# A three-stage kernel: when a gated layer's weights are converted, and in what order

## The chip, the cores and the metric

The kernel runs on one core of a Trainium2 chip. The metric is the device time of one execution in microseconds (us). TensorE (PE) multiplies, VectorE (DVE), ScalarE (ACT) and GpSimd (POOL) work on the elements, and SyncE (SP) issues most of the transfers. Each engine takes its instructions in the order in which they were written; an instruction that waits holds up all behind it on its engine.

## What is computed

Three layers follow each other: causal attention with a cumulative bias, a layer of eight experts (each token goes to one), and a gated layer. The change touches the last one and its surroundings.

```
# x: [2304, 512] from the attention, float32
for e in range(8):                       # w1: [8, 512, 1024], w2: [8, 1024, 512]
    out[mask_e] = gate_w[mask_e] * (relu(x[mask_e] @ w1[e]) @ w2[e])
gate = 1 / (1 + exp(-(out @ w_gate)))    # w_gate, w_val: [512, 1536], float64
val = out @ w_val
y = (gate * val) @ w_out                 # w_out: [1536, 512], float64
```

The three weights of the gated layer come as float64 and are turned into float32 on the chip.

## The kernel before

**Conversion.** `Decode` turns a block of float64 into float32 in four steps on three engines: `near` on POOL (`dn`, line 849) limits the exponent's byte, `far` on DVE (`dd`, 853) takes the difference, `word` on ACT (`ds` or `wr`, 857) writes it as the top of a 32-bit word, and `tail` on DVE (861) puts the mantissa under it. The raw block is tile `dr`, with two buffers; `load` issues the next block's transfer when a block is done.

**Precision.** Products are made from two reduced-precision parts each (high and low): ACT rounds a value to its high part, DVE or POOL subtracts to get the low one, and PE multiplies high by high, high by low and low by high.

**Experts.** Nine slots of 256 tokens, eight steps each. A step of PE makes one block of the hidden layer (`ph`, line 973) and multiplies the block before by w2 (993); ACT and DVE make `hH` and `hL` from `ph`; ACT, DVE and POOL split the weights of three steps further on (`w`, 906 and 909). Then two half-filled slots, four steps each, in plain float32: `half` (1094) transposes the hidden block on PE (`hth`), DVE copies it (`hT`, 1079), and PE multiplies by w2 (1088). `Moe.run` calls `step(u)` after each step, and a table `todo` in the main function says which pieces of the gated layer's preparation are written there.

**Gated layer.** `Moe2` works in units: a block of 512 columns pair by pair (f, six of them), a third of the tokens (t), gate or value (m): 36 units. A unit is a Strassen-like scheme of seven products, `slot` 0 to 6, six matmuls of 384 columns each. Its inputs are the sums of x blocks `a` (lines 1247 to 1249 make seven of them from four raw blocks `xs`, high and low), and of weight blocks `set` (1283 to 1289, from the converted `ds`). ACT copies partial sums out of bank X (`p`, `u`, line 1320), which PE adds to afterwards. `result` writes the gate (`sg`) or the product, which goes to DRAM (`h`, 1340). A dictionary in `run` places the tasks behind slots: `spread(first, last, tasks)` divides a list of them evenly.

**Final product.** `final` (1442) multiplies h, loaded again (`hr`) and split (`hl`, 1430 and 1431), by w_out (`po`), in 72 steps of nine matmuls. Before, the blocks 0 to 2 of w_out are converted in the last units, 3 to 11 from the last unit but one on, one after the other: `load_o` loads five raw blocks (`wr`), and each block's `low` loads the one five further on (line 1404).

Of the kernel before, what the change touches and what calls it, by code (L numbers as in the profile page):

```python
# [815 lines left out]
class Decode:  # L816
# [7 lines left out]
    def __init__(self, tc, pool, srcs):  # L824
        self.nc, self.pool, self.srcs = tc.nc, pool, srcs
        self.raw, self.n, self.i = {}, 0, 0

    def load(self):

        if self.n < len(self.srcs):  # L830
            src = self.srcs[self.n]
            c, w = src.shape[1:]
            t = self.raw[self.n] = self.pool.tile([128, 2048], U8, tag="dr", name="dr", bufs=2)
            self.nc.sync.dma_start(t.rearrange("p (c b) -> p c b", c=c)[:, :, :w], src)
            self.n += 1

    def tasks(self, dst):

        i = self.i
        self.i += 1  # L840
        return self.steps(lambda: self.raw[i], dst, 256) + [lambda: (self.raw.pop(i), self.load())]

    def steps(self, raw, dst, n):
        nc, V, o = self.nc, self.nc.vector, {}
        top = lambda: raw().bitcast(I8).rearrange("p (a b) -> p a b", b=8)[:, :, 4]

        def near():
            o["n"] = self.pool.tile([128, 512], I8, tag="dn", name="dn", bufs=1)[:, :n]
            nc.gpsimd.tensor_scalar(o["n"], top(), 56.0, -56.0, ALU.min, ALU.max)  # L849

        def far():
            o["d"] = self.pool.tile([128, 512], I8, tag="dd", name="dd", bufs=1)[:, :n]
            V.scalar_tensor_tensor(out=o["d"], in0=top(), scalar=-72.0, in1=o["n"], op0=ALU.max, op1=ALU.subtract)  # L853

        def word():
            o["t"] = dst().bitcast(I32)
            nc.scalar.activation(o["t"], o["d"], AF.Copy, scale=float(1 << 27))

        def tail():
            w = raw().bitcast(I32).rearrange("p (a b) -> p a b", b=2)[:, :, 0]  # L860
            V.scalar_tensor_tensor(out=o["t"], in0=w, scalar=5, in1=o["t"], op0=ALU.logical_shift_right, op1=ALU.bitwise_or)  # L861
# [340 lines left out]
class Moe2:  # L1202
# [10 lines left out]
    def __init__(self, tc, moe, x2, ids2, wg, wv, wo, out, hd, keep, rp):  # L1213
        self.tc, self.nc, self.moe = tc, tc.nc, moe
        self.x2, self.ids2, self.out, self.hd = x2, ids2, out, hd
        self.keep, self.rp, self.r = keep, rp, moe.r
# [3 lines left out]
        srcs = [cols(w, f, j, l).rearrange("(c p) b -> p c b", p=128) for f in range(self.NF) for w in (wg, wv) for j, l in blocks]  # L1220
        self.wo = wo.bitcast(U8)
        srcs += [self.wo[128 * f : 128 * f + 128, 2048 * h + 3 : 2048 * h + 2048].rearrange("(c p) b -> p c b", c=1) for f in range(3) for h in range(2)]
        self.dec = Decode(tc, keep, srcs)

# [10 lines left out]
    def load_x(self, t, pool, raws):  # L1235
# [430 lines left out]
```

## Time and profile before

| | us |
|---|---|
| three runs | 1053.5, 1055.35, 1057.93 |
| median | 1055.35 |
| profiled execution | 1056.42 |
| its span, first to last instruction | 1054.3 |
| PE busy | 958.7 (91%) |
| DVE busy | 633.5 (60%) |
| ACT busy | 536.6 (51%) |
| POOL busy | 420.3 (40%) |
| PE's mean granted clock | 0.957 of full |

A share of the whole span says little here, since the three layers have different limits; the stages are read one by one. A row of the timeline is one or more instructions of one kind: start, duration, engine, line, output and input, count, and in brackets the idle time before it and the engine and line that ended it. A matmul's end is modelled, so the time from one start to the next is the better measure of PE's pace.

### The profile page before, as it was taken

What the parts mean: (1) busy time and instruction counts of PE and PEld (TensorE: products, weight loads), DVE (VectorE), ACT (ScalarE), POOL (GpSimd) and SP (SyncE); (2) the same over time, 40 slices, a digit from 0 to 9 for tenths busy, and PEclk for the clock granted to TensorE, in tenths of its full rate; (3) what the DMA queues carried; (4) which work ended last, traced back from release to release, by engine and by line L of the source; (5) the groups of instructions that cost most, each with busy time, mean ns of one, the idle gap of its engine ahead of it and who ended that gap; (6) DMA issues with size and microseconds to landing.
All of it is one profiled execution on the core that took longest, in us unless ns stands there. A gap on an engine that the chain in (4) does not pass through costs nothing. (4 is left out here: it accounts for less than half of the span.)

```text
span 1054.3 us, 18246 instructions
## 1 busy us (share of the span) xinstructions
PE 958.7 (91%) x5937; PEld 866.1 (82%) x5937; DVE 633.5 (60%) x1535; ACT 536.6 (51%) x1317; POOL 420.3 (40%) x642
## 2 busy tenths in 40 slices
PE   7999999998879999999874889999999965899996
PEld 6888888876769999999864788999999954688885
DVE  6899989998565445554163766657576544523320
ACT  6988888887335555555133444353444433322220
POOL 7978697878545556665000000000000023311111
PEclk9999999999889999999987999999999988899998
DMA  6665467885351125115653322314233245434420
GB/s 161 155 136 136 114 78 150 139 99 200 35 62 58 41 81 179 43 41 150 196 165 93 111 67 74 117 62 140 85 109 100 78 165 191 155 130 135 140 76 30
DMA packets 149649, 117.99 MB, mean 112 GB/s; under 512 B 86946, under 2 KB 135357, under 8 KB 149543
## 3 DMA queue, kind: packets, MB, share of 16 engines
q1 hardware_dynamic: 144534, 106.28, 38.9%
q0 software_dynamic: 3792, 10.14, 3.2%
q8 instruction: 49, 0.80, 0.4%
q14 instruction: 58, 0.47, 0.2%
q10 hardware_dynamic: 1216, 0.30, 0.1%
HBM read 112.81 MB, written 29.04 MB: 135 GB/s over the span
## 5 line engine op out<-in xcount | busy, mean ns | idle before, releaser
L1311 PE MATMUL X<-a,set 128*128 128x384 f32 x864 | 173.7, 348 | 26.2 <-ACT u L1320 17.4
L1311 PEld LDWEIGHTS X<-a,set 128*128 128x128 f32 x864 | 155.3, 194 | 34.9 <-ACT u L1320 20.9
L849 POOL TENSOR_SCALAR dn<-dr 128x256 int8<-128x256 int8 x54 | 23.1, 427 | 321.9 <-DVE dd L853 208.6
L1442 PE MATMUL acc<-wo,hl 128*128 128x512 f32 x369 | 91.0, 403 | 14.5 <-ACT hl L1430 13.2
L909 POOL TENSOR_TENSOR w<-raw,w 128x512 fp32r<-128x512 f32 x56 | 78.4, 1410 | 59.1 <-ACT w L906 59.0
L1442 PEld LDWEIGHTS acc<-wo,hl 128*128 128x128 f32 x369 | 70.6, 193 | 32.8 <-ACT hl L1430 14.5
L170 POOL TENSOR_SCALAR bias<-cumB,cumT 128x576 f32<-128x576 f32 (+4 forms) x155 | 82.3, 533 | 37.5 <-DVE nm L289 31.3
L973 PE MATMUL ph<-xT,w 128*128 128x256 f32 x672 | 92.0, 287 | 1.9 <-DVE w L909 1.9
L298 ACT ACTIVATE P<-P,nm 64x64 f32<-64x64 f32 (+4 forms) x160 | 89.7, 564 | 2.9 <-DVE nm L289 2.8
L973 PEld LDWEIGHTS ph<-xT,w 128*128 128x128 f32 x672 | 85.4, 194 | 2.1 <-DVE w L909 2.1
L1311 PE MATMUL Y<-a,set 128*128 128x384 f32 x432 | 82.1, 338 | 0.4 <-DVE a L1248 0.4
L289 DVE CUSTOM_DVE_ANT_0 P<-sb,bias 128x576 f32<-128x576 f32 (+4 forms) x160 | 72.0, 479 | 17.1 <-PE sb L280 11.0
L339 DVE TENSOR_TENSOR PL<-pt,PH 128x512 fp32r<-128x512 f32 (+3 forms) x160 | 78.8, 530 | 3.4 <-ACT PH L331 2.5
L1311 PEld LDWEIGHTS Y<-a,set 128*128 128x128 f32 x432 | 76.6, 190 | 0.8 <-DVE a L1248 0.7
L331 ACT CAST PH<-pt 128x512 fp32r<-128x512 f32 (+3 forms) x160 | 66.9, 466 | 10.2 <-PE pt L317 7.3
L977 ACT ACTIVATE hH<-ph 128x256 fp32r<-128x256 f32 x72 | 27.7, 385 | 86.2 <-PE ph L973 79.6
L317 PE MATMUL pt<-ident,P 128*128 128x128 f32 (+2 forms) x480 | 70.0, 277 | 0.8 <-DVE PL L339 0.7
L978 DVE SCALAR_TENSOR_TENSOR hL<-ph,hH 128x256 fp32r<-128x256 f32 x72 | 30.5, 424 | 58.9 <-ACT hH L977 53.3
L909 DVE TENSOR_TENSOR w<-raw,w 128x512 fp32r<-128x512 f32 x56 | 54.3, 972 | 17.0 <-ACT w L906 14.1
L1449 POOL DMA_INDIRECT out_dram<-oy,row x18 | 19.2, 1068 | 111.4 <-ACT oy L1448 107.7
L906 ACT CAST w<-raw 128x512 fp32r<-128x512 f32 x112 | 63.6, 621 | 0.0
L317 PEld LDWEIGHTS pt<-ident,P 128*128 128x128 f32 (+2 forms) x480 | 53.4, 132 | 12.0 <-issue 6.3
(280 smaller groups left out, 2279.5 us busy)
## 6 DMA issues: line engine op xcount, KB each, us to landing
raw<-in_moe_w_dram SPq DMA_DIRECT2D x80, 512.0 KB
h<-sg SPq DMA_DIRECT2D x72, 192.0 KB
hr<-h SPq DMA_DIRECT2D x72, 192.0 KB
cumB<-cum_d SPq DMA_DIRECT2D x32, 288.0 KB
qraw<-in_q_dram SPq DMA_DIRECT2D x58, 128.0 KB
dr<-in_moe_w_gate_dram SPq DMA_DIRECT2D x24, 255.2 KB
dr<-in_moe_w_val_dram SPq DMA_DIRECT2D x24, 255.2 KB
x<-yt SPq DMA_DIRECT2D x9, 512.0 KB
```

The costliest lines, as they stand in the source:

```text
L170: (nc.vector if n in FILLB else nc.gpsimd).tensor_scalar(res[i][:rows], cumB[:rows, :m], -1.0, self.cumT[:rows, i, n : n + 1], ALU.mult, A ...
L289: nc.vector.tensor_tensor_reduce(out=pt[:rows], in0=self.sb[:rows, o : o + m], in1=self.bias_t[n][i][:rows], op0=ALU.add, op1=ALU.min, sca ...
L298: nc.scalar.activation(h["P"][i][:rows], h["P"][i][:rows], AF.Exp, bias=h["nm", i][:rows], scale=-1.0, accum_out=self.sums_t[(n // 2) % 3] ...
L317: nc.tensor.transpose(pt[: TS[j], c : c + TS[i]], h["P"][i][: TS[i], T0[j] : T0[j] + TS[j]], self.ident[: TS[i], : TS[i]])
L331: nc.scalar.copy(t[:r, a:z], pt[:r, a:z])
L339: nc.vector.tensor_tensor(t[:r, a:z], pt[:r, a:z], h["H"][u][:r, a:z].bitcast(F32), ALU.subtract)
L906: nc.scalar.copy(v, src)
L909: (eng or nc.vector).tensor_tensor(v, src, h.bitcast(F32), ALU.subtract)
L973: nc.tensor.matmul(ph, w[:, 128 * dc : 128 * dc + 128], x[:, dc], start=k == 0, stop=k == 11)
L978: nc.vector.scalar_tensor_tensor(out=hL, in0=ph, scalar=0.0, in1=hH.bitcast(F32), op0=ALU.max, op1=ALU.subtract)
L1311: self.nc.tensor.matmul(bank, w[:, c], a[:, h, c], start=first and k == 0, stop=k == 5, skip_group_check=True)
L1442: nc.tensor.matmul(self.acc[t], h[:, a, 128 * t : 128 * t + 128], w, start=f == 0 and k == 0, stop=f == 11 and k == 2)
```

## The change

Four things change.

1. **w_out is converted during the expert slots.** All twelve blocks are loaded, converted (512 columns at a time, three raw buffers) and stored to a DRAM tensor `wo32` as float32. In the end they are loaded from there, split into high and low, and used; no conversion is left in the last units.
2. **The first gate and value weights are converted there too**, behind the blocks of w_out, not among the half-filled experts.
3. **The steps of a conversion lie apart**: `stages` returns `near`, `far`, `word` and `tail`, each written behind a slot of its own, two conversions interleaved; the load of the next raw block follows `tail`. Buffers of `dn` and `dd` go from one to two. The second set's sums are all made in the first unit.
4. **Loads and stores are reordered**: the raw x of both remaining thirds is loaded at the start of the units; a store of h is written one slot later; eight blocks of h are loaded ahead of the final product instead of four; every second low half of w_out is made on DVE instead of POOL.

```
     def last_weight(self, pool):
+        dec = Decode(self.tc, pool, 512, [self.wo[128 * f : 128 * f + 128, 3:].rearrange("(c p) b -> p c b", c=1) for f in range(12)], 3)
+        for _ in range(3):
+            dec.load()
+        new = lambda: pool.tile([128, 512], F32, tag="dt", name="dt", bufs=2)
+        return [dec.stages(new, lambda t, f=f: self.nc.sync.dma_start(self.wo32[128 * f : 128 * f + 128, :], t)) for f in range(12)]
...
+        for k, stages in enumerate(glu.last_weight(pool(wo_ctx, "dec", side="right", reuse_waits="tile"))):
+            for i, task in enumerate(stages):
+                put(2 * k + i - 55, [task])
+        put(-28, [wo_ctx.close, open_xs, glu.dec.load, glu.dec.load])
+        (d0, s0), (d1, s1) = glu.w_tasks(0, lambda: xs[0]), glu.w_tasks(1)
+        for k, stages in enumerate(d0 + d1):
+            for i, task in enumerate(stages):
+                put(2 * k + i - 27, [task])
...
-                2: x[:4], 3: x[4:9] + d0[:5], 4: x[9:13] + d0[5:15], 5: x[13:] + d0[15:], 6: s0 + b0 + d1[:5], 7: d1[5:] + s1, 8: [glu.preload],
+            put(3, x[:4])
+            put(4, x[4:7] + s0[0])
...
-            for m, first, last in ((0, (b + (4 if f == 1 else 3), 5), (b + 5, 5)), (1, (b + 6, 5), (b + 8, 4))):
-                spread(first, last, [x for w in self.w_tasks(m) for x in w])
+            for m, soon, there in ((0, at(b + 1, 5), at(b + (4 if f == 1 else 3), 5)), (1, at(b + 4, 5), at(b + 6, 5))):
...
+                for stages, k in zip(blocks, (0, 1, 7, 8)):
+                    for i, task in enumerate(stages):
+                        put(soon + k + i, [task])
...
-        spread((n - 2, 4), (n - 2, 4), [lambda: [self.load_o(f) for f in range(3, 8)]])
-        spread((n - 2, 6), (n - 1, 3), ot[3] + ot[4])
+        put(at(n - 2, 5), [self.load_o])
+        put(at(n - 1, 0), [lambda: [self.load_h(0, f) for f in range(8)]])
```

What this does to the order is shown at three places. First, DVE among the half-filled experts, before; `a` and `xs` are x's high-low work, `hT` is the copy that PE waits for, `dd` and `ds` are a conversion:

```order
L1071 COPY xTh<-htr 128x512
L1248 TENSOR_TENSOR a_0_8774<-xs_8770,a_0_8774 128x768
L1079 COPY hT<-hth 128x256
L1248 TENSOR_TENSOR a_2_8776<-xs_8771,a_2_8776 128x768
L1249 TENSOR_TENSOR xs_8771<-xs_8773,xs_8771 128x768
L1248 TENSOR_TENSOR a_1_8775<-xs_8772,a_1_8775 128x768
L1249 TENSOR_TENSOR xs_8773<-xs_8770,xs_8773 128x768
L1249 TENSOR_TENSOR xs_8770<-xs_8771,xs_8770 128x768
L853 SCALAR_TENSOR_TENSOR dd<-dr,dn 128x256
L861 SCALAR_TENSOR_TENSOR ds<-dr,ds 128x256
L1079 COPY hT<-hth 128x256
```

The same place on DVE now:

```order
L1071 COPY xTh<-htr 128x512
L1079 COPY hT<-hth 128x256
L1257 TENSOR_TENSOR a_0_8969<-xs_7656,a_0_8969 128x768
L1079 COPY hT<-hth 128x256
L1257 TENSOR_TENSOR a_2_8971<-xs_7657,a_2_8971 128x768
L1258 TENSOR_TENSOR xs_7657<-xs_7659,xs_7657 128x768
L1257 TENSOR_TENSOR a_1_8970<-xs_7658,a_1_8970 128x768
L1079 COPY hT<-hth 128x256
L1295 TENSOR_TENSOR set<-ds,set 128x2x256
L1258 TENSOR_TENSOR xs_7659<-xs_7656,xs_7659 128x768
L1258 TENSOR_TENSOR xs_7656<-xs_7657,xs_7656 128x768
L1079 COPY hT<-hth 128x256
```

One more copy of `hT` stands ahead of the first use of x, and no conversion stands between two copies.

Second, DVE at the start of the units, before; `set` is the second weight set, `sg` and `p` are results:

```order
L1330 TENSOR_TENSOR sg<-Z,p_11909 128x384
L1286 TENSOR_TENSOR set<-ds,set 128x2x256
L1248 TENSOR_TENSOR a_0_11888<-xs,a_0_11888 128x768
L1286 TENSOR_TENSOR set<-ds,set 128x2x256
L1248 TENSOR_TENSOR a_2_11890<-xs,a_2_11890 128x768
L1249 TENSOR_TENSOR xs<-xs 128x768
L1330 TENSOR_TENSOR sg<-Y,u_11954 128x384
```

The same place on DVE now:

```order
L1340 TENSOR_TENSOR sg<-Z,p_12029 128x384
L1295 TENSOR_TENSOR set<-ds,set 128x2x256
L1295 TENSOR_TENSOR set<-ds,set 128x256
L1298 TENSOR_TENSOR ds<-ds 128x256 x4
L1295 TENSOR_TENSOR set<-ds,set 128x2x256
L1340 TENSOR_TENSOR sg<-Y,u_12076 128x384
L1295 TENSOR_TENSOR set<-ds,set 128x2x256
L1257 TENSOR_TENSOR a_0_12004<-xs,a_0_12004 128x768
```

The whole of the second set's sums stands there now, ahead of x's work.

Third, SP at the end, before; `wr` is a raw block of w_out, `hr` a block of h for the final product, `h` a store:

```order
L1376 DMA wr<-in_moe_w_out_dram 128x4093 x5
L1340 DMA h_1_98<-sg 128x384
L1424 DMA hr_14639<-h_0_64 128x384
L1424 DMA hr_14639<-h_0_67 128x384
L1424 DMA hr_14639<-h_0_70 128x384
L1424 DMA hr_14639<-h_0_73 128x384
L1340 DMA h_2_96<-sg 128x384
L1376 DMA wr<-in_moe_w_out_dram 128x4093
L1340 DMA h_1_95<-sg 128x384
L1376 DMA wr<-in_moe_w_out_dram 128x4093
```

The same place on SP now:

```order
L1350 DMA h_0_95<-sg 128x384
L1388 DMA wr<-wo_64 128x512 x12
L1350 DMA h_0_98<-sg 128x384
L1419 DMA hr_14704<-h_0_65 128x384
L1419 DMA hr_14704<-h_0_68 128x384
L1419 DMA hr_14704<-h_0_71 128x384
L1419 DMA hr_14704<-h_0_74 128x384
L1419 DMA hr_14709<-h_0_77 128x384
```

All twelve blocks of w_out are loaded in one piece ahead of eight blocks of h, and no load of `wr` stands behind a store any more.

## Rows read from the trace of the kernel before

**Rows 1.** Windows by stage: busy us (instructions), granted clock, DMA share, GB/s.

```profile
350.00:510.40 160.40, 160.40 (x1345) 160.40 (x1344) 76.97 (x119) 85.27 (x180) 98.98 (x79) 1.00 0.31 96
510.40:571.30 60.90, 39.08 (x227) 35.11 (x225) 26.70 (x51) 18.09 (x35) 3.68 (x8) 0.83 0.48 148
571.30:612.20 40.90, 32.42 (x151) 29.94 (x151) 25.86 (x36) 19.35 (x34) 0.00 (x0) 0.88 0.34 98
612.20:656.50 44.30, 39.38 (x212) 37.92 (x212) 27.02 (x58) 19.32 (x43) 3.28 (x8) 0.96 0.27 84
656.50:844.00 187.50, 185.14 (x1051) 181.64 (x1050) 121.35 (x256) 85.41 (x192) 13.67 (x32) 1.00 0.30 97
844.00:918.30 74.30, 48.90 (x196) 39.25 (x194) 37.12 (x61) 24.70 (x49) 24.35 (x26) 0.82 0.51 171
918.30:1045.40 127.10, 127.04 (x556) 104.27 (x556) 33.15 (x67) 30.45 (x70) 16.81 (x16) 1.00 0.31 106
```

**Rows 2.** Chain of waits: start us, us, what; products of a unit.

```profile
671.26 2.08 PE X L1311 x12
```

**Rows 3.** Timeline of PE, half-filled experts: start, us, what, [idle before].

```profile
513.52 0.38 PE L1077 MATMUL hth<-ident,hh 128*128 128x128 f32 x2
...
517.25 0.38 PE L1077 MATMUL hth<-ident,hh 128*128 128x128 f32 x2
...
528.20 3.78 PE L1088 MATMUL yh<-hT,raw 128*128 128x128 f32 x16 [4.67 <-DVE hT L1079]
...
564.77 3.78 PE L1088 MATMUL yh<-hT,raw 128*128 128x128 f32 x16 [7.09 <-DVE tbl L1230]
571.26 2.29 PE L1311 MATMUL X<-a,set 128*128 128x384 f32 x6 [2.71 <-ACTq L1057]
```

**Rows 4.** Timeline of ACT, the same stretch.

```profile
525.99 0.83 ACT L1247 CAST a<-xs 128x768 fp32r<-128x768 f32 x1 [6.20 <-DMA xs<-x]
...
568.59 0.58 ACT L1005 COPY yt<-yh 128x512 f32<-128x512 f32 x1 [3.61 <-PE yh L1088]
```

**Rows 5.** Groups by line, expert stage: xcount, busy us, mean ns, idle before.

```profile
L909 POOL TENSOR_TENSOR w<-raw,w 128x512 fp32r<-128x512 f32 x52 | 73.4, 1420 | 52.4 <-ACT w L906 52.2
...
L909 DVE TENSOR_TENSOR w<-raw,w 128x512 fp32r<-128x512 f32 x52 | 47.0, 904 | 14.7 <-ACT w L906 11.9
```

**Rows 6.** Tile wr, 512 columns: ns min/median/max, first and last start.

```profile
L849 POOL TENSOR_SCALAR dn<-wr x9: 625/636/947, 865.0 to 912.8; 128x512 int8<-128x512 int8 x9
L853 DVE SCALAR_TENSOR_TENSOR dd<-wr,dn x9: 684/691/693, 865.6 to 913.7; 128x512 int8<-128x512 int8 x9
L857 ACT ACTIVATE wr<-dd x9: 629/630/632, 866.4 to 914.5; 128x512 int32<-128x512 int8 x9
```

**Rows 7.** Instructions on tile dr, 256 columns.

```profile
L853 DVE SCALAR_TENSOR_TENSOR dd<-dr,dn x54: 414/420/429, 532.8 to 859.1; 128x256 int8<-128x256 int8 x54
```

**Rows 8.** Groups of DVE by line, first units.

```profile
L1248 DVE TENSOR_TENSOR a<-xs,a 128x768 fp32r<-128x768 f32 x13 | 12.4, 955 | 9.5 <-ACT a L1247 9.3
...
L1330 DVE TENSOR_TENSOR sg<-Z,p 128x384 f32<-128x384 f32 x3 | 1.7, 553 | 10.4 <-PE Z L1311 10.4
```

**Rows 9.** Timeline of DVE, its first row in the units.

```profile
575.09 0.56 DVE L1330 TENSOR_TENSOR sg<-Z,p 128x384 f32<-128x384 f32 x1 [10.37 <-PE Z L1311]
```

**Rows 10.** Timeline of PE, units 3 and 6.

```profile
608.46 1.15 PE L1311 MATMUL X<-a,set 128*128 128x384 f32 x5 [0.31 <-DVE a L1248]
...
629.99 2.36 PE L1311 MATMUL X<-a,set 128*128 128x384 f32 x12 [2.65 <-ACT u L1320]
```

**Rows 11.** Timeline of PE, the first steps of the final product.

```profile
896.28 4.21 PE L1442 MATMUL acc<-wo,hl 128*128 128x512 f32 x9 [10.66 <-ACT hl L1430]
```

**Rows 12.** Timeline of SP, the loads at the end.

```profile
860.94 3.40 SPq L1376 DMA_DIRECT2D wr<-in_moe_w_out_dram  x5
...
864.91 2.53 SPq L1424 DMA_DIRECT2D hr<-h  x4
```

**Rows 13.** Windows of 5 us at the end, the one with most DMA.

```profile
870.00:875.00 5.00, 4.40 (x20) 3.54 (x18) 4.13 (x6) 3.32 (x8) 2.15 (x3) 0.88 1.00 382
```

More of the change, by code (lines that the diff above doesn't have):

```diff
@@ L1398, in high @@
             self.po[f] = (t[:, 0:512], t[:, 512:1024])
-            nc.scalar.copy(self.po[f][0], full())
-        def low():
-            nc.gpsimd.tensor_tensor(self.po[f][1], full(), self.po[f][0].bitcast(F32), ALU.subtract)
-            if 3 <= f and f + 5 < 12:
-                self.load_o(f + 5)
-        if f < 3:
-            dec = sum((self.dec.tasks(lambda h=h: full()[:, 256 * h : 256 * h + 256]) for h in range(2)), [])
-        else:
-            dec = self.dec.steps(lambda: self.scr[f][:, :1024], full, 512)
@@ L1434, in final @@
+        return [high, low]
     def final(self, g, f):
@@ L1495, in run @@
+        put(at(2, 2), [lambda: self.room_x(2, self.ap)])
+        spread(at(2, 3), at(3, 4), self.x_tasks(2, raws[1]))
+        put(at(5, 0), [self.rows()])
+        free = 0
         for f in range(1, NF):
             b = 6 * f - 6
-            for m, first, last in ((0, (b + (4 if f == 1 else 3), 5), (b + 5, 5)), (1, (b + 6, 5), (b + 8, 4))):
-                spread(first, last, [x for w in self.w_tasks(m) for x in w])
-        ot = [self.o_tasks(f) for f in range(12)]
-        spread((n - 3, 5), (n - 2, 4), sum(ot[:3], []))
@@ L1507, in run @@
                 self.slot(u, s)
-                for task in todo.pop(7 * u + s, []):
+                for task in todo.pop(7 * u + s, []) + now:
                     task()
@@ L1516, in run @@
                 self.slot(n, (2, 4)[q])
-            elif q == 3:
+            if q == 1:
+                for store in self.late:
+                    store()
+            if q == 7:
                 a_ctx.close()
                 self.hp = P(ctx, "o_h")
-            while q >= 3 and loaded < min(q + 12, len(steps)):
+            while q >= 7 and loaded < min(q + 12, len(steps)):
                 self.load_h(*steps[loaded])
                 loaded += 1
-            if 5 <= 4 + q < 12:
-                for task in ot[4 + q]:
-                    task()
-            while split < min(q + 4, loaded):
+            while split < min(q + 3, loaded):
                 for task in self.h_tasks(*steps[split]):
```

210 lines of the change are left out of this document (119 added, 91 removed).

## The prediction

> **What bounds the kernel now.** I read the table of stages first [rows 1]. Each of its rows is a stretch of the span with every engine's busy time, the granted clock and the DMA share. TensorE (PE) is busy for all of the expert stage (350 to 510.4 us: 160.40 of 160.40 at clock 1.00), and nearly so in the long middle of the gated layer (656.5 to 844) and in the last product (918.3 to 1045.4). The time is lost in four other stretches. To size each I divide by PE's full pace. One of the 42 products' matmuls of a unit costs 2.08 / 12 = 0.173 us [rows 2], so a unit of 42 costs 7.28 us; one matmul of the final product costs 127.1 / 556 = 0.229 us [rows 1].
>
> - 510.4 to 571.3, half-filled experts: one step takes 517.25 - 513.52 = 3.73 us while nothing waits, but PE waits 4.67 and 7.09 us for VectorE (DVE), which copies hT, at a mean clock of 0.83 [rows 1, 3].
> - 571.3 to 612.2, first units: 151 matmuls x 0.173 = 26.2 us of work in 40.9; 14.7 lost.
> - 612.2 to 656.5: 212 x 0.173 = 36.8 in 44.3; 7.5 lost.
> - 656.5 to 844: 25 units x 7.28 = 182.0 in 187.5; 5.5 lost.
> - 844 to 918.3: 102 product matmuls and 92 final ones, 17.7 + 21.0 = 38.7 us in 74.3; 35.6 lost, one wait alone being 10.66 us, for ACT's hl [rows 11].
>
> So the bound is the order in which DVE, ACT, POOL and SP do the conversion around PE, not the amount of it. What the change can give back is in these stretches, and what it puts into the expert stage stands beside a PE that has no idle time.
>
> **Expert slots: conversions added.** Twelve conversions of 512 columns and eight of 256 now lie among the slots. One of 512 costs POOL 0.64, DVE 0.69 twice and ACT 0.63 us [rows 6]; one of 256 costs DVE 0.42 twice [rows 7], and I take the same 0.42 for its POOL and ACT steps. DVE gets 24 x 0.69 + 16 x 0.42 = 23.3 us, POOL 12 x 0.64 + 8 x 0.42 = 11.0, ACT 10.9. They were busy for 77.0, 99.0 and 85.3 of 160.4 us [rows 1], so DVE goes to 100, POOL to 110, ACT to 96: all fit. PE waits for them only through hH and hL (one step ahead) and the split weights (three steps ahead). On SP each load and store of a conversion waits for its last DVE step, with the expert loads queued behind it; those wait for splits that come later still on DVE. A gain is excluded, since PE is always busy at full clock. The low end is 0; the high end, each of the 40 DVE instructions costing PE a whole POOL subtraction of 1.42 us [rows 5], is 57 us. I take +1, near the low end, because DVE keeps 60 us of idle time there.
>
> The row shows what such neighbours cost each other: the split on DVE averages 0.904 us beside POOL's 1.42, while an instruction of the same width takes 0.69 [rows 5, 6]. [...]
>
> **Half-filled experts.** The eight conversions leave this stretch, and the first use of x moves a step later, behind one more hT. The x loads land as before, since what they wait for (the last full slot's store) has not moved: ACT's first cast starts at 525.99 and ends at 526.82 [rows 4]. From there DVE's order up to the last hT holds ten instructions of 0.955 (taken from the same line in the units) [rows 8], one of 0.69 and ten of 256 columns at 0.42: 14.4 us, so 541.3, plus about 1 us of waits for ACT, 542.3. PE's own pace would be ready at 513.52 + 7 x 3.73 + 0.9 = 540.5, so DVE is late by a little. The last yh takes half a step (1.8 us), to 544; ACT's copy yt is held by three more DVE instructions (2.3 us) and the table load, and ends near 545.5. Before, the copy ended at 568.59 + 0.58 and the units began at 571.26, 2.1 us later [rows 3, 4]; so they begin at about 548 instead of 571.3: 23 us. I take **21**, keeping 2 us for waits on ACT that the sum leaves out. Ends: 14 (half of the waits come back at the clock of 0.83) and 25.
>
> **First units.** x for both remaining thirds is loaded at once, which removes the waits for xs. But DVE has more to do here: eight instructions of the second set (three of 0.69, five of 0.42: 4.2 us) instead of two (1.4), and six conversion steps (2.5). Up to the product that waits for the last third's S2, DVE's order is: second set 4.2, 18 x-instructions at 0.955 (17.2), thirteen of a unit's results at 0.55 (7.2) [rows 8], conversions 2.5: 31.1 us, beginning 3.8 us in as now (575.09 - 571.26 [rows 3, 9]). That makes 34.9 us at best, against 608.46 - 571.26 = 37.2 before [rows 3, 10]. With 2 us of waits for casts (9.3 us of them stood before this line [rows 8]) almost nothing is left: **0**, ends -4 and +6. What is late next is DVE itself.
>
> **Units 4 to 8.** PE waited 2.65 us for u here, behind conversion steps queued on ACT, each waiting for DVE's [rows 10]. Now the steps of one conversion lie a slot apart and are done earlier. Of 7.5 us lost I take **-5.5** (0 to -7). **Middle:** the 5.5 us are spread over 25 units, some before a conversion, some in every unit; I take the part that the conversions cause as **-2** (-5 to +2).
>
> **The end.** Nine of twelve blocks of w_out were loaded and converted from 861 us to 916, one after the other, with four engines in turn and the load of a later block waiting for an earlier one [rows 6, 12]; all of this is gone. What remains per block is a load, an ACT cast and one subtraction. At the seam, PE waits for the last copy of X and the first cast of h (about 1 us), then for two results and the first low half on DVE (about 1); the loads may cost 1 to 2; the last units keep 0.2 each. I take 5 us lost instead of 35.6: **-30.5** (-22 to -33).
>
> **Sum.** +1 - 21 + 0 - 5.5 - 2 - 30.5 = -58. The profiled execution took 1056.42 us (span 1054.3 and 2.1 around it), 1.07 above the median of the three runs (1055.35). 1056.42 - 58 = 998.4; at the median, 997.
>
> **Rivals.**
> - *The loads at the seam take the place of the conversions.* Twelve wr loads (0.262 MB each) and eight hr loads (0.197) go out in one piece: 4.7 MB, at 382 GB/s [rows 13] 12.3 us; SP's issue at 0.63 to 0.68 us each [rows 12] takes 13 us. By the order they begin in the last unit but one, some 10 us (one unit of 7.3 and a part of the one before) ahead of the first use of h. If h comes 4 us late and later ones follow at the pace of the issue, with the clock falling as it did at 844 to 918.3 (0.82), some 12 us of the gain go: 1009. For it: h stands behind all of w_out on SP. Against: the first eight h were stored long before, and wait for nothing but the queue.
> - *DVE stays the bound in the first units.* The old order held 25.2 us of DVE work in 33.4, by the same sum: 8.2 idle. With that idle time beside 31.1 the product waits until 43.1 instead of 37.2, and the lag eats the 5.5 of units 4 to 8: +11, 1008.
> - *Every wait goes:* -23 at the halves, -4, -7, -5, -33: 983.
> - *Slower: the expert slots stall.* If DVE's conversion steps come between hH and hL and each holds PE for over 58 / 40 = 1.45 us, the gain is gone; at 2 us each, 80 us, it would be 1076. A wait of DVE for a late POOL step could do it, at the slots where POOL also gathers rows. Against: a step (24 matmuls at 160.4 / 1345) takes 2.86 us and leaves DVE half of it idle, 83.4 of 160.4 [rows 1], and hL is needed only one step on.
> - *The steps apart do nothing:* the in-order queues wait as long at other places, and only the removed final conversions count for half: 1040; it is the case nearest to no change.
>
> [...]
>
> **How the numbers follow.** Forecast 997 (own range 986 to 1006): 0.55. Loads at the seam 0.14, DVE in the first units 0.12, every wait gone 0.09, nothing from the steps apart 0.04, slower 0.04, and 0.02 for no measurable change. A measurement of this kernel can tell about 0.5% from no change. Range 979 to 1020: it takes in both partial cases and the best one. Faster by over 0.5%: 0.94; within: 0.02; slower: 0.04.
>
> **What would show it.** Right: the expert stage still without PE idle time; no PE wait over 2 us for hT; the first unit about 38 us after the expert stage; about 41 us for units 0 to 3 with DVE busy over three quarters of it; less than 6 us lost between the last set and the final product, with no hl wait of over 3 us. Wrong: PE waits for hL or w below 510 us (slots); a wait for hr at the seam (loads); units 0 to 3 in 30 us or 50 us (DVE's sum was not the bound).

## The result, and the profile after

The changed kernel takes 993.04 us (median of four runs, 990.48 to 998.86); the kernel before, on the same chip, 1055.3. The ratio is 0.9416, 95% interval 0.937 to 0.9462. The forecast was 997, its range 979 to 1020. The profiled execution took 992.62 us, its span 990.9.

First the table of stages, as in [rows 1]. Columns: stretch, its length, then busy us (instructions) of PE, PE's weight loads, DVE, ACT and POOL, granted clock, DMA share, GB/s.

```profile
346.30:514.80 168.50, 165.90 (x1374) 164.39 (x1373) 121.14 (x161) 97.61 (x207) 117.18 (x101) 1.00 0.51 163
514.80:552.90 38.10, 32.49 (x227) 30.06 (x225) 17.54 (x29) 14.04 (x25) 0.00 (x0) 1.00 0.54 181
552.90:591.20 38.30, 32.00 (x151) 29.63 (x152) 32.23 (x51) 21.40 (x40) 2.24 (x3) 0.87 0.43 131
591.20:627.80 36.60, 36.60 (x211) 36.30 (x210) 24.15 (x52) 18.65 (x41) 2.85 (x6) 1.00 0.23 74
627.80:810.20 182.40, 182.40 (x1053) 182.31 (x1052) 118.47 (x252) 85.39 (x191) 14.25 (x30) 1.00 0.30 97
810.20:842.00 31.80, 28.23 (x140) 25.80 (x139) 18.72 (x31) 12.42 (x26) 6.46 (x5) 0.95 0.65 224
842.00:982.00 140.00, 139.92 (x613) 114.52 (x611) 37.30 (x74) 34.44 (x78) 18.14 (x17) 1.00 0.35 117
```

The first number behind the length is PE's busy time; read it against the length. In rows 4 and 5 (units 4 to 33) PE is now busy all the time, which it was not in [rows 1]. In the first row it is not, and there it was busy for every microsecond before.

For a balance that closes I cut both traces at the same instructions of PE: the second `ph` made with split weights `w` (346.39 us before, 346.33 after), the first half-filled product `phh`, the first product of the units, the starts of product Z in units 4, 9 and 34 (counted from 0), and the start of the last copy `oy`. Every run of the study is read by these marks. The forecast in the last column is that of the prediction.

| stage, us | before | after | change | forecast |
|---|---|---|---|---|
| expert steps | 163.97 | 168.50 | +4.5 | +1 |
| half-filled experts | 60.90 | 38.03 | -22.9 | -21 |
| units 0 to 3 | 43.07 | 40.37 | -2.7 | 0 |
| units 4 to 8 | 44.10 | 36.68 | -7.4 | -5.5 |
| 25 units of the middle | 187.68 | 182.35 | -5.3 | -2 |
| end | 199.28 | 169.70 | -29.6 | -30.5 |
| sum | | | -63.4 | -58 |

What stands ahead of the first mark (-0.1) and behind the last one (0) makes no difference.

Half-filled experts, PE's timeline (start, us, engine, line, operation, names and shapes, and in brackets the idle time before and what ended it). Where [rows 3] had waits of 4.67 and 7.09 us, 0.91 and 1.97 are left, and sixteen matmuls take 2.05 us instead of 3.78:

```profile
532.64 2.05 PE L1088 MATMUL yh<-hT,raw 128*128 128x128 f32 x16 [0.91 <-DVE hT L1079]
548.07 2.05 PE L1088 MATMUL yh<-hT,raw 128*128 128x128 f32 x16 [1.97 <-DVE hT L1079]
552.86 1.31 PE L1321 MATMUL X<-a,set 128*128 128x384 f32 x6 [2.73 <-ACTq L1057]
```

Units 0 to 3, the same view, the waits over half a microsecond. It is the one place among the units where PE still waits for DVE and ACT; where [rows 10] had 2.65 us in unit 6, there is no wait:

```profile
570.59 3.36 PE L1321 MATMUL X<-a,set 128*128 128x384 f32 x12 [2.28 <-ACT u L1330]
577.55 1.50 PE L1321 MATMUL X<-a,set 128*128 128x384 f32 x7 [0.87 <-ACT u L1330]
583.53 1.97 PE L1321 MATMUL Z<-a,set 128*128 128x384 f32 x5 [2.93 <-DVE a L1257]
```

The seam, in the chain of work that ended last (start, us, what). The 10.66 us that PE waited for `hl` [rows 11] are gone; the one wait left is 3.57 us before `acc`, and the chain tells whose it is: the last piece of SP's row of loads, twelve of w_out and then h.

```profile
816.03 0.38 SPq L1388
...
818.37 5.03 DMA wr<-wo
...
823.49 5.45 DMA hr<-h
...
828.96 0.52 ACT h L1433
...
829.52 3.09 PE acc L1449 x9
```

The expert steps, PE's timeline, the three longest waits. All are for `hL`, and none stood there before:

```profile
363.54 0.38 PE L993 MATMUL sb<-hL,w 128*128 128x256 f32 x1 [0.23 <-DVE hL L978]
...
389.09 0.38 PE L993 MATMUL y<-hL,w 128*128 128x256 f32 x1 [0.71 <-DVE hL L978]
...
415.13 0.39 PE L993 MATMUL sb<-hL,w 128*128 128x256 f32 x1 [1.40 <-DVE hL L978]
```

Together they are 2.3 us. The whole 4.5 shows in the time from one step's start to the next: laid beside the kernel before, eight of the 55 steps are longer, by 0.2 to 1.7 us, and the others are the same.

### The profile page after: what moved, and what is told of

Same layout as the page of the kernel before. It is cut to its first block, busy times and chain, and to the rows that moved or that the text cites. A ratio compares the mean times of both kernels' runs of the same rounds, so it can differ in the third digit from the quotient of the medians.

```text
span 990.9 us, 18243 instructions
## 1 busy us (share of the span) xinstructions
PE 938.4 (95%) x5937; PEld 855.2 (86%) x5937; DVE 654.9 (66%) x1535; ACT 535.0 (54%) x1314; POOL 420.1 (42%) x633
## 5 line engine op out<-in xcount | busy, mean ns | idle before, releaser
L1321 PE MATMUL X<-a,set 128*128 128x384 f32 x864 | 166.9, 341 | 6.1 <-ACT u L1330 3.1
L845 POOL TENSOR_SCALAR dn<-dr 128x256 int8<-128x256 int8 (+1 forms) x60 | 34.9, 582 | 259.0 <-DMA dr<-in_moe_w_gate_dram 111.6
L1449 PE MATMUL acc<-set,hl 128*128 128x512 f32 x333 | 77.4, 389 | 0.0
L1449 PEld LDWEIGHTS acc<-set,hl 128*128 128x128 f32 x333 | 62.5, 188 | 13.2
L1455 DVE COPY oy<-acc 128x512 f32<-128x512 f32 x6 | 4.2, 692 | 97.3 <-PE acc L1449 97.3
L1330 ACT COPY u<-X 128x384 f32<-128x384 f32 x72 | 34.5, 480 | 59.3 <-PE X L1321 59.3
L909 DVE TENSOR_TENSOR w<-raw,w 128x512 fp32r<-128x512 f32 x56 | 58.8, 1052 | 11.2 <-ACT w L906 10.4
```

What stands on the lines that cost most here:

```text
L909: (eng or nc.vector).tensor_tensor(v, src, h.bitcast(F32), ALU.subtract)
L1321: self.nc.tensor.matmul(bank, w[:, c], a[:, h, c], start=first and k == 0, stop=k == 5, skip_group_check=True)
L1330: self.nc.scalar.copy(t, self.o[u, "X"])
L1449: nc.tensor.matmul(self.acc[t], h[:, a, 128 * t : 128 * t + 128], w, start=f == 0 and k == 0, stop=f == 11 and k == 2)
```

## The experiments

All are edits of the changed kernel but the eighth, which is one of the kernel before. In the expectations "slot" ahead of the half-filled experts means one of PE's steps of 2.88 us (up to 3.31 where x is transposed). Stages by the marks above, from one profile each; totals as the ratio to the kernel before, run on the same chip, because the chips differ (the kernel before took 1055.3, 1052.45, 1062.43, 1059.79 and 1057.49 us in the five batches). Runs of one batch shared a chip and the runs of the kernel before on it.

| run | batch | expert steps | half-filled | units 0-3 | 4-8 | middle | end | ratio (95%) |
|---|---|---|---|---|---|---|---|---|
| before | 1 | 163.97 | 60.90 | 43.07 | 44.10 | 187.68 | 199.28 | 1 |
| after | 1 | 168.50 | 38.03 | 40.37 | 36.68 | 182.35 | 169.70 | 0.9416 (0.937 to 0.9462) |
| e1, no w_out conversion | 2 | 163.98 | 39.39 | 41.60 | 37.31 | 182.55 | 170.98 | 0.942 (0.94 to 0.944) |
| e2, x a step earlier | 2 | 168.10 | 44.13 | 40.71 | 36.52 | 182.39 | 168.58 | 0.9474 (0.9451 to 0.9497) |
| e3, conversions back | 2 | 168.50 | 50.75 | 41.60 | 37.31 | 182.49 | 169.12 | 0.9562 (0.953 to 0.9594) |
| e4, steps together | 2 | 168.48 | 39.92 | 44.22 | 37.55 | 185.74 | 170.98 | 0.9489 (0.9458 to 0.952) |
| e5, converted later | 3 | 168.16 | 38.31 | 39.74 | 36.91 | 182.57 | 169.76 | 0.9391 (0.9359 to 0.9424) |
| e6, loads in fours | 3 | 167.76 | 42.60 | 41.04 | 37.32 | 182.37 | 167.93 | 0.9367 (0.9334 to 0.94) |
| e7, x on GpSimd | 3 | 168.53 | 39.69 | 43.71 | 37.04 | 182.40 | 168.82 | 0.9414 (0.9372 to 0.9457) |
| e8, before, nine not converted | 3 | 163.96 | 60.41 | 44.00 | 44.33 | 188.25 | 184.54 | 0.9862 (0.9811 to 0.9912) |
| e9, after again | 4 | 168.09 | 37.98 | 40.57 | 37.28 | 182.55 | 169.74 | 0.9413 (0.9387 to 0.9438) |
| e10, tail a step later, fours | 4 | 172.24 | 37.83 | 40.56 | 37.22 | 182.35 | 166.40 | 0.9417 (0.9393 to 0.9442) |
| e11, thinner, x pressed, fours | 4 | 165.77 | 38.22 | 47.28 | 36.51 | 182.42 | 166.39 | 0.9403 (0.9376 to 0.943) |
| e12, thinner, fours | 5 | 165.71 | 37.97 | 40.65 | 37.27 | 182.39 | 166.41 | 0.9345 (0.9315 to 0.9374) |

Stages that an edit doesn't touch show how far one profile can be trusted: 0.2 us in the middle, 0.8 in the expert steps and in units 4 to 8, 1.2 in units 0 to 3, 2 to 2.5 in the half-filled experts and the end (e6, whose profile was the longest of its five executions, 4.6 in the half-filled experts).

**e1. What the conversion of w_out costs among the experts.**

```
-        for k, stages in enumerate(glu.last_weight(pool(wo_ctx, "dec", ...))):
-            for i, task in enumerate(stages):
-                put(2 * k + i - 55, [task])
...
-            self.nc.sync.dma_start(self.scr[f], self.wo32[128 * f : 128 * f + 128, :])
+            self.nc.sync.dma_start(self.scr[f], self.moe.w1[f // 4, 128 * (f % 4) : 128 * (f % 4) + 128, 0:512])
```

> The changed kernel without the conversion of w_out in the experts' slots (24 DVE, 12 POOL and 12 ACT instructions of 512 words and 24 transfers less; the last product is fed with other words of the same size, so the conversion of w_out is what this run leaves out). My theory: the expert slots grew by 3.0 us over the kernel before (168.2 to 171.2) because these DVE instructions take 1.3 us instead of 0.69 beside GpSimd's subtractions, and so the full experts go back to 168.2 +-0.7 and the kernel to about 990 (-3), with DVE's w instructions (978 ns in mean) back at 904. Rival, that the order of the stage or the drift ahead of it made the 3 us: the stage stays at 171 and the kernel at 993. Nothing changes behind the slots in either case: 38 us of half-filled experts, 172 us of end.

The expert steps take 163.98 us, the 163.97 of the kernel before to a hundredth. So w_out's conversion costs 4.5 us there, not 3.0 (that figure began at an earlier mark; from there to the one used here PE's clock was 0.60 before, 342.2 to 346.4 us, and 1.00 after, 343.6 to 346.3) and not the 1 of the forecast. The total did not follow: 0.942 is the changed kernel's ratio. In the profile the half-filled experts (+1.4), units 0 to 8 (+1.9) and the end (+1.3) gave the 4.5 back, each within what these stages scatter; whether by chance or because work that begins earlier meets its loads earlier, this run does not tell.

**e2 and e3. What made the half-filled experts short.** In e2:

```
-            put(3, x[:4])
-            put(4, x[4:7] + s0[0])
+            for f in x[:4]:
+                f()
+            put(3, x[4:7])
+            put(4, x[7:10] + s0[0])
```

(and so on). In e3, with the eight conversions taken out of the expert steps:

```
-            put(3, x[:4])
-            put(4, x[4:7] + s0[0])
-            put(5, s0[1] + x[7:10])
+            put(3, x[:4] + d0[0])
+            put(4, x[4:7] + d0[1] + s0[0])
+            put(5, d0[2] + s0[1] + x[7:10])
```

> The changed kernel with the high and low parts of the first third of the tokens one step earlier among the half-filled experts, as the kernel before had them. My theory: part of the 22.9 us that left this stretch came from the moved x work, which stood ahead of hT on DVE; with it back the waits for hT of 0.91 and 1.97 us grow, and the stretch goes from 38.0 to 40-42 us, the kernel to 995-997. Rival, that the x work never mattered and only the conversions in these steps did: 38.0 +-0.5, kernel 993.

> The changed kernel with the eight conversions of the first weight back among the half-filled experts (as in the kernel before, in eight pieces of four steps) and no longer in the expert slots from 427 us on. My theory: these conversions made the stretch of 60.9 us; it grows from 38.0 by 10 to 20 us, the expert slots lose less than 0.5 us because 256-word conversions cost nothing there, and the kernel goes to 1003-1013. Rival, that the longer stretch came from the order of x work and of the DMA loads: 38 to 42 us, kernel 993-997.

Both parts count: +6.1 us for x a step earlier (more than the 2 to 4 expected), +12.7 for the conversions (inside 10 to 20). PE's timeline shows the same wait, for `hT` on DVE, in both. Of e2, the first wait, longer than the 0.91 of the changed kernel:

```profile
531.76 3.78 PE L1088 MATMUL yh<-hT,raw 128*128 128x128 f32 x16 [4.46 <-DVE hT L1079]
```

Of e3, the three longest:

```profile
536.00 2.05 PE L1088 MATMUL yh<-hT,raw 128*128 128x128 f32 x16 [3.21 <-DVE hT L1079]
...
547.03 2.85 PE L1088 MATMUL yh<-hT,raw 128*128 128x128 f32 x16 [2.73 <-DVE hT L1079]
...
559.35 3.78 PE L1088 MATMUL yh<-hT,raw 128*128 128x128 f32 x16 [4.12 <-DVE hT L1079]
```

The two sum to 18.8 of the 22.9 us. Both rows with 3.78 us follow a wait of over 4 us. In the kernel before, the rows with 3.78 us behind waits of 4.67 and 7.09 [rows 3] ran at a granted clock of 0.50 (528.2 to 532.0 and 564.8 to 568.5 us); elsewhere in e2 sixteen of these matmuls take 1.95 to 2.05. So these waits cost a second time, in PE's pace behind them, and the two causes together may well cost more than one by one; the two at once were not run, and the other 4.1 us are not put down to anything. In e3 the expert steps kept 168.50 us without the conversions of 256 columns, so those cost nothing there, and the 4.5 us are all w_out's.

**e4. The four steps of a conversion in one slot of the units.**

```
-                    for i, task in enumerate(stages):
-                        put(soon + k + i, [task])
+                    put(soon + k + 3, stages)
```

> The changed kernel with the four steps of each conversion in the units put into one slot (the slot of the last step), nothing else moved. My theory: steps apart keep DVE from standing in line for POOL and ACT; together they return the kernel before's losses of the 25 middle units (187.7 instead of 182.3 us) and some of units 4 to 8 (36.7, was 44.2): middle +3 to +5, units 4 to 8 +1 to +4, the kernel 997-1002. Rival, that the loss was of the raw loads' and stores' order and of the weight's start far ahead of its use: middle +0 to +1, kernel 993-994.

The middle goes to 185.74, 3.4 of the 5.3 us; units 0 to 3 lose 3.9, which was not expected; units 4 to 8 lose 0.9 of 7.4, less than the least expected and hardly more than the scatter of 0.8. So setting the steps apart made most of the gain of the middle. In units 4 to 8 it made little: most of that gain comes with the rest of the new order, the conversions begun units earlier and the second set made in unit 0, which this run left as it was; that part was not tried by itself.

**e5. Fewer conversions in units 1 and 2.**

```
-                soon = max(soon, free)
+                soon = max(soon, free) if f > 1 or m else at(3, 0)
```

> The changed kernel with the conversions of the second weight's first half begun in unit 3 instead of unit 1. In units 1 to 3 DVE is busy 9.5 to 9.6 of 10 us and the four units take 38.3 us where 29.2 would do without waits. My theory: DVE's sum sets these units, so 4 to 6 conversions less (1.2 us of DVE each) take 2 to 4 us from them; units 4 to 8 then give back up to 1 us; kernel 990-992. Rival, that the x work and the ACT evictions' order set these units and DVE only fills up: 38.3 +-0.7, kernel 993.

Units 0 to 3 take 39.74 us against 40.37 and 40.57 in the two traces of the changed kernel. Theory: 2 to 4 less; rival: within 0.7. By the number the rival holds, but the run is a weak test. Of the conversions only two of four left these units, not four to six: DVE's busy time over them fell from 32.95 us to 31.95. The stage gave back 0.6 to 0.8 us, less than its scatter of 1.2, so whether the sum of DVE's work sets it stays open. The total (0.9391) lies 0.2% under the changed kernel's, less than the intervals tell apart.

**e6. The last loads in fours.**

```
-        put(at(n - 2, 5), [self.load_o])
-        put(at(n - 1, 0), [lambda: [self.load_h(0, f) for f in range(8)]])
+        put(at(n - 2, 5), [lambda: self.load_o(0, 4), lambda: [self.load_h(0, f) for f in range(4)], lambda: self.load_o(4, 8)])
+        put(at(n - 1, 0), [lambda: [self.load_h(0, f) for f in range(4, 8)], lambda: self.load_o(8, 12)])
```

> The changed kernel with SP's last loads in another order: four of w_out, four of h, four of w_out, four of h, four of w_out, instead of twelve of w_out and then eight of h. In the trace of the changed kernel the first product of the end waits 3.57 us for ACT's copy of h, which waits for the load of h (5.45 us in the chain) that stands behind the twelve of w_out. My theory: with four loads ahead of h instead of twelve the wait falls to 0-1 us: -2.5 to -3.5, kernel 989.5-990.5. Rival, that the loads of h can't come earlier because their stores end last (the last h of a row is stored in the last unit), or that w_out then comes late: -0.5 to +2, kernel 992.5-995.

The wait at the seam falls from 3.57 us to 0.98 and 0.68, and the end from 169.70 to 167.93, then to 166.40, 166.39 and 166.41 in the three later runs that have this order: 1.8 to 3.3 us. So h's place behind twelve loads on SP made 1.9 of the 3.57 us of waiting, and the stores of h did not hold it. The rest of the 3.3 goes with PE's pace behind that wait. Over the next 20.5 us the granted clock was 0.92 in the changed kernel, and its first nine `acc` matmuls took 3.09 us; in e9 nine took 3.89 and in e6 seven took 3.10, but in e10, e11 and e12 seven took 1.88, 1.88 and 1.89. That is why e6, with the same short waits, gained 1.8 in its profile, less than the 2.5 to 3.5 expected; what slowed its matmuls is not shown. PE's timeline of e12:

```profile
827.31 0.73 PE L1449 MATMUL acc<-set,h 128*128 128x512 f32 x2 [0.98 <-ACT h L1433]
...
828.73 1.89 PE L1449 MATMUL acc<-set,h 128*128 128x512 f32 x7 [0.68 <-DVE h L1437]
```

**e7. Three of the seven low parts of x, for two thirds of the tokens, on GpSimd.**

```
-        L = lambda i: lambda: nc.vector.tensor_tensor(...)
+        L = lambda i: lambda: (nc.gpsimd if t and i in (self.A22, self.S1, self.S4) else nc.vector).tensor_tensor(...)
```

> The changed kernel with three of the seven low parts of the second and third third of the tokens (of the x work in units 1 to 3) on GpSimd instead of DVE. My theory from the sums: DVE loses 6 instructions of about 0.95 us, 5.7 us of the 38.3 us in which it is the bound: -2 to -4 us. [...]

It goes the other way: units 0 to 3 come to 43.71, 3.3 us longer, with six instructions, 5.7 us of work, taken from DVE (the total, 0.9414, does not show the loss). DVE is busy for 34.97 us there, against 32.95 in the changed kernel: it got nothing back. Two timelines show what it met. DVE:

```profile
586.74 0.95 DVE L1257 TENSOR_TENSOR a<-xs,a 128x768 fp32r<-128x768 f32 x1
587.61 0.54 DVE L1347 TENSOR_TENSOR u<-Y,u 128x384 f32<-128x384 f32 x1
588.19 1.60 DVE L1349 TENSOR_TENSOR sg<-u,sg 128x384 f32<-128x384 f32 x1
```

and POOL at the same time:

```profile
584.70 1.83 POOL L1257 TENSOR_TENSOR a<-xs,a 128x768 fp32r<-128x768 f32 x1 [3.77 <-ACT a L1256]
586.91 2.47 POOL L1257 TENSOR_TENSOR a<-xs,a 128x768 fp32r<-128x768 f32 x1 [0.37 <-ACT a L1256]
```

The last DVE row, two inputs from SBUF, takes 0.56 us in the changed kernel; here it begins beside POOL's subtraction of 586.91 and ends 0.41 us after it. The row before it, whose Y comes from PSUM, lies wholly beside the same subtraction and keeps its 0.54. POOL needs 1.83 us for what DVE does in 0.95, and 2.47 where it began beside DVE's own subtraction of 586.74. How much of the 3.3 us is DVE's longer instructions and how much POOL's longer time was not divided.

**e8. How much of the end was conversion.** In the kernel before:

```
-            return self.scr[f][:, 1024:]
+            return self.scr[f][:, :512]
...
-            dec = self.dec.steps(lambda: self.scr[f][:, :1024], full, 512)
+            dec = []
```

with raw blocks of another weight, 4096 bytes a row for 4093, in the loads.

> The kernel before without the conversion of nine of the twelve weights of w_out in its last units and at its end (its raw words are replaced by as many of another weight, used as they are; the conversion is what this run leaves out; loads keep their size, place and order). The end took 201.4 us before and 171.8 after. My theory: about 25 of the 29.6 us are the conversions and their waits, so the end comes to 173-179 us and the kernel to 1027-1033. Rival, that the order of the loads and the places in memory that they wait for made most of it: the end stays at 190-200 us, the kernel at 1045-1053.

(The expectation's 201.4 and 171.8 begin at another mark, 2.1 us earlier; the difference is the same.) Neither: the end comes to 184.54, half of the way (14.7 of 29.6 us; the ratio 0.9862 says the same, 1.38% of 1062.43 is 14.7, by its interval 9 to 20). PE's waits of over 0.3 us in the end fall from 25.3 to 12.6 us in sum. The ones that stay, PE and then ACT, show the other half:

```profile
858.37 3.19 PE L1311 MATMUL X<-a,set 128*128 128x384 f32 x12 [2.66 <-ACT u L1320]
...
868.88 2.29 PE L1311 MATMUL X<-a,set 128*128 128x384 f32 x6 [2.58 <-ACT p L1320]
...
890.96 4.21 PE L1442 MATMUL acc<-wo,hl 128*128 128x512 f32 x9 [4.03 <-ACT hl L1430]
```

```profile
856.41 0.42 ACT L857 ACTIVATE ds<-dd 128x256 int32<-128x256 int8 x1 [1.89 <-DVE dd L853]
...
867.84 0.62 ACT L1399 CAST wo<-wr 128x512 fp32r<-128x512 f32 x1 [2.90 <-DMA wr<-in_moe_w_dram]
...
890.39 1.50 ACT L1430 CAST hl<-hr 128x384 fp32r<-128x384 f32 x3 [11.18 <-DMA hr<-h]
```

The first is still a conversion (blocks 0 to 2 of w_out kept theirs). The other two are loads: ACT stands in its row behind a copy that waits for a block of w_out, and later behind h, whose loads stood on SP behind four stores of h (875.05 to 884.42 us). After those waits PE's clock was 0.85 in mean over 843 to 900 us. So the gain at the end has two halves: the conversions of nine blocks, and, by these rows, the place of the loads and the conversions of the other three, with the clock of 0.85 behind them. The second half was not divided further; the low halves moved from POOL to DVE are in it too.

**e9 to e12. The expert steps and the seam.** e9 is the changed kernel once more. e10:

```
-            for i, task in enumerate(stages):
+            for i, task in zip((0, 1, 2, 4), stages):
                 put(2 * k + i - 55, [task])
```

e11 and e12 (what follows behind is moved by four steps), and x in e11 alone:

```
-                put(2 * k + i - 55, [task])
+                put(5 * k // 2 + i - 55, [task])
...
-        spread(at(1, 0), at(2, 2), self.x_tasks(1, raws[0]))
+        spread(at(1, 0), at(2, 0), self.x_tasks(1, raws[0]))
...
-        spread(at(2, 3), at(3, 4), self.x_tasks(2, raws[1]))
+        spread(at(2, 1), at(3, 2), self.x_tasks(2, raws[1]))
```

All three have the loads in fours of e6.

> The changed kernel as it is, beside the two that follow on the same chip, so that their totals and stages have a measure there. Every theory expects the stages of its first trace within 1 us each (expert slots from the second slot of raw weights to the first half-filled expert 168.5; half-filled experts 38.0; end 169.7 from the Z of the last unit but one to the last copy), except the half-filled experts and units 0 to 3, where PE's clock fell after waits and 2 us more may come; ratio to the kernel before 0.937 to 0.946.

> The changed kernel with the last step of w_out's conversions in the experts' slots one slot later, so that DVE has one of these instructions in every slot instead of two in every other one; and with SP's last loads in the order four of w_out, four of h, four, four, four. The expert slots took 4.5 us more than without the conversion, all of it in three places where the slots have a transposition as well. Theory that DVE runs over in single slots, where two conversion steps and xT stand beside each other: the stage goes from 168.5 to 165-167 us. Rival, that each DVE step waits out GpSimd's subtractions wherever it stands (3.41 us for one step while GpSimd's w ran), so that spreading moves the waits but not their sum: 168-170 us. The end, by the loads' order, 1.5 to 2 us shorter than in the changed kernel (169.7 to 167.9 in an earlier run) in both cases.

> The changed kernel with w_out's conversions begun every 2.5 slots instead of every 2 (the first weight's follow 4 slots later), the x work of the second and third third of the tokens pressed together into 8 slots each instead of 10 and 9, and the last loads in four and fours. Theory of single overfull slots: 20 percent fewer conversion steps per slot meet the transpositions less often, expert slots 166-167.5 us; rival, that the waits for GpSimd's subtractions come with every step: 168-169. Units 0 to 3 (40.4 us from the first product to the Z of unit 4): if the x work waits for its place in the order, -1 to -3 us; if for the loads and the chain ACT to DVE, 0 to +1; if the evictions behind it come late, +1 to +3. End as in the run before: 1.5 to 2 us shorter than in the changed kernel.

> The changed kernel with w_out's conversions begun every 2.5 slots instead of every 2 and the last loads in four and fours; the x work as the changed kernel has it. From the stages of the runs that had these parts: expert slots 165.8 us from the second slot of raw weights (168.1 to 168.5 in the changed kernel), end 166.4 (169.7), everything else as in the changed kernel (half-filled experts 38, units 0 to 3 40.5, units 4 to 8 37, middle 182.4). That is -6 us: ratio to the kernel before 0.935 to 0.937, where the changed kernel had 0.9416 and 0.9413. Rival, that the gains are given back where the DMA and the clock set the time (the half-filled experts and the first units, whose x comes by the stores of the expert stage): ratio 0.940 to 0.942.

e9 repeats every stage within 0.6 us. e10 is worse than either theory: 172.24. PE waited for `hH`, which is ACT's, and ACT's timeline gives the cause, nine times in twelve, five of them over 2 us:

```profile
404.33 0.63 ACT L853 ACTIVATE dt<-dd 128x512 int32<-128x512 int8 x1 [3.75 <-DMA wo<-dt]
...
420.07 0.63 ACT L853 ACTIVATE dt<-dd 128x512 int32<-128x512 int8 x1 [4.14 <-DMA wo<-dt]
```

A later `tail` makes a later store, and with two buffers `dt` the next `word` on ACT waits for that store to land, with `hH` behind it. In the changed kernel this happens once (2.17 us). What e10 was to tell apart, it does not tell.

e11 and e12 do: with 2.5 steps for a conversion instead of 2 the expert steps take 165.77 and 165.71, 2.3 to 2.8 less; one wait for `hL` of 0.85 to 0.87 us and one of 0.20 are left. That is what the theory of overfull steps expected, though the conversion's DVE instructions also grew shorter (1.18 us in mean, 1.34 in the changed kernel), so that the two are not wholly apart. Pressing x together costs 6.7 to 6.9 us in units 0 to 3 (47.28): PE waits up to 4.30 us for ACT's `u`, which stands on ACT behind the x work. e12 has the two gains alone: 0.9345 of the kernel before (989.18 against 1057.49 us), where the changed kernel has 0.9416 and 0.9413. Its ratio is the lowest of the study, by what its two stages give (2.4 to 2.8 and 3.3 us); the intervals set it apart from the changed kernel's repeat e9, not from e6.

## Why the prediction was right, step by step

**Half-filled experts: right**, -22.9 for -21. The first unit starts 38.03 us after the stage began; 38 was named, and no wait for `hT` is over 2 us. The sum itself had 23, of which the prediction kept back 2. e2 and e3 show that both named causes count, and the waits for `hT` in them that DVE's order was the right thing to add up.

**End: right in size, too simple in cause.** -29.6 for -30.5, one wait of 3.57 us left of the 5 us allowed. The prediction took loads and conversions "one after the other" as one chain and did not divide it; e8 shows that the conversions of nine blocks are half, 14.7 us. The rival of the loads at the seam came true in its first part: h was late behind w_out by 3.57 us, where it had 4, and that wait was one of the prediction's signs of being wrong. Its second part did not come: no later load was waited for, and the clock behind the wait was 0.92, not 0.82, so that the price was 3.3 us by e10 to e12, not 12.

**Expert steps: the term that was mis-sized**, +4.5 for +1, inside its ends of 0 and 57. Its sign of being wrong came true, PE waits for `hL` below 510 us. Two steps of the prediction failed: the price of a DVE instruction beside POOL, and that DVE's idle time over the whole stage pays for it. For the price it had two figures: the mean of the split weights, 0.904 us against 0.69 [rows 5, 6], which is 0.21 more, and as its high end a whole POOL subtraction of 1.42 us [rows 5]. The trace of after, first to last of w_out's conversions; minimum, median and maximum ns:

```profile
L978 DVE SCALAR_TENSOR_TENSOR hL<-ph,hH x26: 409/412/425, 348.5 to 427.5; 128x256 fp32r<-128x256 f32 x26
```

```profile
L849 DVE SCALAR_TENSOR_TENSOR dd<-dr,dn x12: 677/1768/1784, 352.1 to 423.3; 128x512 int8<-128x512 int8 x12
```

```profile
L858 DVE SCALAR_TENSOR_TENSOR dt<-dr,dt x12: 679/1304/3406, 359.7 to 427.9; 128x512 int32<-128x512 int32 x12
```

The 24 instructions of the conversion take 1.34 us in mean, 0.65 more than the 0.69 of [rows 6], not 0.21. Laid beside POOL's timeline, twenty of them overlap with a POOL instruction and four do not; the four take 0.68 us each. In four traces (after, e3, e9, e11) all fourteen without overlap take 0.68. Each of the twenty ends 0.54 to 0.66 us after the end of a POOL instruction, hardly less than the 0.68 that it takes alone, as if it had waited that one out. One place, DVE:

```profile
410.13 3.41 DVE L858 SCALAR_TENSOR_TENSOR dt<-dr,dt 128x512 int32<-128x512 int32 x1
413.46 0.68 DVE L849 SCALAR_TENSOR_TENSOR dd<-dr,dn 128x512 int8<-128x512 int8 x1
414.06 0.68 DVE L909 TENSOR_TENSOR w<-raw,w 128x512 fp32r<-128x512 f32 x1
414.67 0.41 DVE L978 SCALAR_TENSOR_TENSOR hL<-ph,hH 128x256 fp32r<-128x256 f32 x1
...
417.90 1.78 DVE L849 SCALAR_TENSOR_TENSOR dd<-dr,dn 128x512 int8<-128x512 int8 x1
```

and POOL:

```profile
409.83 2.55 POOL L909 TENSOR_TENSOR w<-raw,w 128x512 fp32r<-128x512 f32 x2
412.34 0.64 POOL L845 TENSOR_SCALAR dn<-dr 128x512 int8<-128x512 int8 x1
415.92 3.22 POOL L909 TENSOR_TENSOR w<-raw,w 128x512 fp32r<-128x512 f32 x2 [2.94 <-ACT w L906]
```

The first DVE row spans three POOL instructions and ends 0.56 us after the last; the second meets none. And `hL`, with one input from PSUM (`ph`) and one from SBUF, never grew (0.409 to 0.425 us), though those at 416.20, 421.70 and 425.18 us began while a POOL subtraction ran.

e7 gives a second place. What lets the one engine hold up the other these rows do not show: the 3.41 us also span two POOL instructions that began after the DVE row, the second of the two at 409.83 and the one at 412.34.

The 0.21 rests on the mean of [rows 5], and that mean hides two cases that stand side by side in the trace of before. DVE:

```profile
386.98 0.68 DVE L909 TENSOR_TENSOR w<-raw,w 128x512 fp32r<-128x512 f32 x1
...
388.20 1.16 DVE L909 TENSOR_TENSOR w<-raw,w 128x512 fp32r<-128x512 f32 x1
```

and POOL:

```profile
387.45 3.06 POOL L909 TENSOR_TENSOR w<-raw,w 128x512 fp32r<-128x512 f32 x2 [1.95 <-ACT w L906]
```

The first DVE row began 0.47 us ahead of POOL and did not grow; the second began while POOL was at work and did. Of the 52 instructions 33 take 0.68 to 0.69 us, 25 of them begun with no POOL instruction running; 19 take 1.09 to 1.84, and every one of these ended 0.55 or 0.56 us after the end of a POOL instruction. So 0.21 was the mean of 33 that paid nothing and 19 that paid 0.4 to 1.2 us. Of w_out's 24 conversion steps 18 grew by over 0.1 us.

By the sum DVE still had the time, as the prediction said: it was busy for 121 of 168.5 us. What the sum does not show is the place. In the rows above, the `hL` for which PE waited 1.40 us at 415.13 stands on DVE right behind the 3.41, a second conversion step and a weight; with 0.68 in place of 3.41 it could have been ready 2.7 us sooner. The eight longer steps lie at three places in the stretch, five of them among the steps that also transpose (`xT`) and three two steps behind. e12 gets 2.8 of the 4.5 back by a wider spacing alone.

**Units 0 to 3: right within its ends, its reason neither shown nor refuted.** -2.7 for 0 (-4 to +6). The sum took DVE as what is late, and its signs are there: 40.4 us where about 41 was named, DVE busy for 32.2 of 38.3 us. PE's longest wait (2.93) is for DVE's `a`. The next (2.28) is for ACT's `u`, and `u` stands on ACT behind a cast of x that waited for DVE:

```profile
569.33 0.83 ACT L1256 CAST a<-xs 128x768 fp32r<-128x768 f32 x1 [0.34 <-DVE xs L1258]
570.07 0.47 ACT L1330 COPY u<-X 128x384 f32<-128x384 f32 x1
```

No run proves it: e5 took only 1.0 us of DVE's busy time away and gained 0.6, in e7 DVE's time did not fall. e11, with the same work sooner and 6.9 us lost, shows that the order counts beside the sum; the clock (0.87) is below full as well. Which link of the chain DVE, ACT, PE ends it was not tried.

**Units 4 to 8 and the middle: right in sign, short by 1.9 and 3.3.** The prediction took only a part where it could not divide the loss. PE lost 7.5 and 5.5 us there; nearly all of both is gone. In the middle e4 gives 3.4 of 5.3 to the steps lying apart.

**The rivals.** The slower one had its mechanism (the expert steps' waits for `hL`) and not its price: 4.5 / 40 = 0.11 us for each of the 40 DVE instructions, against a break-even of 1.45 (0.19 if only the 24 of w_out's are counted). That DVE stays the bound of the first units and gives 11 us back did not come. "Every wait goes" is nearest to the truth for the units; it gave 983.

## To carry to other kernels

Work that fits by the sum of busy times still has a price where it stands: put beside a full engine, look at the fullest step of the cycle, at what each instruction meets on the other engine, and at how many buffers its stores have to land in. Before giving work to another engine, find rows in which the two engines run at once, and take the instructions that began while the other engine was at work, not the mean of the group. And when a stage is shortened, ask what was queued behind it: half of the end's gain here did not come with the nine conversions taken out.

## What was not expected of the hardware

A DVE instruction with two inputs from SBUF took 3.41 us instead of 0.68 beside three POOL instructions in a row, two of which began after it, and ended 0.56 us after the last; the next `dt` step, at 416.53, took 1.45 us and ended 0.55 us after the first of two, while the second was running. And wider spacing (e11), which left the number of instructions as it was, cut the `dt` steps' mean only from 1.32 to 1.06 us, but the stage's loss from 4.5 to 1.8: so it counts where the long ones fall.
